# A new whole-kernel order table for sliding-window attention with a convolutional feed-forward: convolution kinds, lead-in and buffers changed with it

## The chip, the cores and the metric

The kernel runs on one core of one Trainium2 chip. The metric is the device time of one execution in microseconds (us), taken on that core. With each execution comes the mean clock that the throttle granted to the matrix engine, as a share of full speed. Engine names follow the profile: PE is TensorE, DVE is VectorE, ACT is ScalarE, POOL is GpSimd, SP is the engine that issues most transfers.

Executions of one kernel differ by up to about 1.4% within a batch here, and the granted clock explains little of it: in the batch of e5 to e8 the unchanged kernel took 227.31 us at a mean clock of 1.000, 227.10 us at 0.992 and 229.90 us at 0.978. Differences under 1% between kernels are therefore not read below. A run more than 1.5% above the fastest of its kernel counts as slow, and is left out of the ratios.

## The reference, cut to what matters

```python
# q, k, v: (8 batches, 8 heads, 576 rows, 64); w_in (512, 1024), conv_w (3, 1024), w_out (1024, 512); float32
def attention(q, k, v):
    scores = q @ k.T / sqrt(64)
    scores = where(abs(i - j) <= 32, scores, -1e9)
    attn = exp(scores - max);  attn /= sum(attn) + 1e-9
    return attn @ v                                  # heads then side by side: x (8, 576, 512)

def ffn(x):
    h = maximum(x @ w_in, 0)
    conv = sum(conv_w[t] * shifted(h, t - 1) for t in range(3))    # along the 576 rows, zeros outside
    return (h / (1 + exp(-conv))) @ w_out            # (8, 576, 512) float32
```

The 8 x 576 rows of the feed-forward are cut into 12 chunks of 384 rows, and its 1024 columns into 8 blocks of 128. A *unit* is one block of one chunk: its matmul, a relu into a buffer `hT`, three *taps* of the convolution, a tanh and a gate. Chunk 1 is done in halves, so there are 104 units.

## The kernel before

The kernel has no scheduler. It describes every operation with what it reads and writes, and a hand-tuned table gives the order, the engine and the buffer of each. Each engine then executes its own instructions in the order of the table, so what stands at the head of a queue holds up all behind it.

```python
BUFS = {'st': 3, 'qkb': 5, 'qkT': 3, 'attn': 2, 'rec': 4, 'xn': 3, 'hT0': 8, 'hT1': 6, 'hT2': 6, 'cp': 2, 'gT': 4, 'y': 7}
CONV = (                     # one letter for each unit, a row for each chunk
    '33333333',
    '33q3323r23223321',
    's222r32q',
    # [...] nine more rows
)
ORDER = """
15D 11D0 12D 1F 17D 2F 13D1 2F 14D 7F 28G 0V 1P0 2F 2V 33V 1F 4G 4F 20G0 21S 2F 16D 5G 1F 22S1 41P120 42P 23S 3G
[...]                        # operation number, engine (D: SP, P, V: DVE, S: ACT, G: GpSimd), buffers; 7F: 7 warming matmuls
"""
TAPS = {                     # kind: taps on (PE, GpSimd, DVE)
    "3": ((0, 1, 2), (), ()), "2": ((0, 2), (), (1,)), "1": ((0,), (), (1, 2)),
    "q": ((), (0, 2), (1,)), "r": ((), (0,), (1, 2)), "s": ((0,), (1, 2), ()),
}
```

The four pieces of code are inside a unit. `hT` and `cp` are in SBUF, `pc` is a bank of PSUM (called `pf` in the profile):

```python
            def emit_times(e_, cp, kk):              # a product on GpSimd: 384 columns, SBUF to SBUF
                gpsimd.tensor_scalar(
                    out=in3(cp.ap), in0=taps(kk), scalar1=w_tap(kk), scalar2=0.0, op0=ALU.mult, op1=ALU.add
                )

            def emit_add(e_, cps=cps):               # kinds q and s: the two products added, on GpSimd
                gpsimd.tensor_tensor(out=in3(cps[0].ap), in0=in3(cps[0].ap), in1=in3(cps[1].ap), op=ALU.add)

            def emit_pc(e_, on_pe=on_pe):            # taps as matmuls with a diagonal, into PSUM
                for kk in on_pe:
                    tensor.matmul(pc.ap[:, 0:nc_], diag_w[:, kk, m, :], taps(kk), ...)

            def emit_tap(e_, kk, from_):             # a tap on DVE; from_ is pc (PSUM) or a product cp (SBUF)
                vector.scalar_tensor_tensor(
                    out=in3(pc.ap), in0=taps(kk), scalar=w_tap(kk), in1=in3(from_.ap), op0=ALU.mult, op1=ALU.add,
                )
```

A unit of kind q costs GpSimd two products and an add, and DVE one tap with two inputs in SBUF (`hT` and `cp`). A unit of kind 2 costs PE two matmuls, and DVE one tap with one input in SBUF (the other is PSUM).

The softmax here doesn't subtract the row's maximum and nothing guards it: scores larger than these inputs give would overflow.

## Time and profile before

| | before |
|---|---|
| time, median of 3 | 227.27 us (227.18 to 227.44) |
| span of the profiled execution | 225.6 us, mean clock 0.991 |
| DVE taps that add a GpSimd product | 35, mean 0.618 us |
| GpSimd products, and adds of two products | 63, mean 0.622 us; 24, mean 1.016 us |
| GpSimd's waits for DVE taps to free a product buffer | 17.0 us |

Columns: line, engine, operation, output<-inputs, shape, count | busy us, mean ns | idle just before, and what ended it.

```profile
L232 POOL TENSOR_SCALAR cp<-hT,conv_w_sb 128x384 f32<-128x384 bf16 (+1 forms) x63 | 38.9, 622 | 46.1 <-ACT hT L232 20.2
...
L232 POOL TENSOR_TENSOR cp<-cp,cp 128x384 f32<-128x384 f32 (+1 forms) x24 | 24.4, 1016 | 1.6
L232 DVE TENSOR_TENSOR attn<-attn,mask 128x1152 bf16<-128x1152 bf16 x26 | 23.0, 886 | 2.4 <-ACT attn L232 2.3
...
L232 DVE SCALAR_TENSOR_TENSOR pf<-hT,conv_w_sb,cp 128x384 f32<-128x384 bf16 (+1 forms) x35 | 21.2, 618 | 0.0
```

The last line is the tap that adds a product: DVE never waits for one (0.0), and the mean of 630 ns for its 33 full-width ones is close to the 613 ns of a full-width tap on PSUM. And from the view of waits of the same kernel (what waited for what: us in total, times, longest):

```profile
POOL cp L232 <- ACT hT L232: 20.2, 10, 4.1
POOL cp L232 <- DVE pf L232: 17.0, 15, 4.2
ACT pf L232 <- DVE pf L232: 11.1, 18, 1.2
```

With only two product buffers, GpSimd stands still 17.0 us until a DVE tap has read a product.

### The profile page before, as it was taken

What the parts mean: (1) busy time and instruction counts of PE and PEld (TensorE: products, weight loads), DVE (VectorE), ACT (ScalarE), POOL (GpSimd) and SP (SyncE); (2) the same over time, 40 slices, a digit from 0 to 9 for tenths busy, and PEclk for the clock granted to TensorE, in tenths of its full rate; (3) what the DMA queues carried; (4) which work ended last, traced back from release to release, by engine and by line L of the source; (5) the groups of instructions that cost most, each with busy time, mean ns of one, the idle gap of its engine ahead of it and who ended that gap; (6) DMA issues with size and microseconds to landing.
All of it is one profiled execution on the core that took longest, in us unless ns stands there. A gap on an engine that the chain in (4) does not pass through costs nothing.

```text
span 225.6 us, 7189 instructions
## 1 busy us (share of the span) xinstructions
PE 211.5 (94%) x2720; PEld 122.9 (54%) x2720; DVE 197.3 (87%) x467; ACT 187.5 (83%) x474; POOL 137.7 (61%) x203
## 2 busy tenths in 40 slices
PE   7698899989989999989999998999999999999993
PEld 5366567658555655545555454545655565455541
DVE  6279869899999979797999788989999999899990
ACT  2689899998989889879889989689989999777642
POOL 5978654654376937695368736756386735566640
PEclk9889999999999999999999999999999999999999
DMA  6999999999989999999997989994535212501224
GB/s 201 331 285 358 355 266 281 321 308 253 290 170 324 317 175 287 236 306 224 288 347 129 202 278 358 182 231 147 144 36 118 99 46 49 175 1 49 93 101 178
DMA packets 66391, 48.16 MB, mean 214 GB/s; under 512 B 50781, under 2 KB 50805, under 8 KB 66357
## 3 DMA queue, kind: packets, MB, share of 16 engines
q1 hardware_dynamic: 64992, 46.32, 78.6%
q10 hardware_dynamic: 1364, 1.39, 2.9%
q8 instruction: 21, 0.34, 0.8%
q14 instruction: 14, 0.11, 0.2%
HBM read 32.52 MB, written 9.44 MB: 186 GB/s over the span
## 4 chain that ended last, share of the span: by engine, by line
PE 41%; DVE 18%; ACT 17%; DMA 13%; issue 5%; SPq 3%; POOL 2%; DVEq 0%; ACTq 0%; POOLq 0%
PE pf L232 41%; DMA st<-in_k_dram 7%; ACT attn L232 6%; DVE pf L232 5%; DVE gT L232 4%; SPq L232 3%; DMA out_dram<-y 3%; ACT xn L232 3%; DVE qkT L232 2%; ACT pf L232 2%; DMA vo<-ve 2%; DVE attn L232 2%; DVE xn L232 2%; ACT qkb L232 2%; ACT y L232 1%
## 5 line engine op out<-in xcount | busy, mean ns | idle before, releaser
L232 PE MATMUL pf<-xT,w_in_sb 128*128 128x385 bf16 (+2 forms) x416 | 73.4, 315 | 3.6 <-ACT hT L232 0.9
L232 PE MATMUL pf<-w_out_sb,gT 128*128 128x512 bf16 x288 | 72.2, 380 | 0.0
L232 POOL TENSOR_SCALAR cp<-hT,conv_w_sb 128x384 f32<-128x384 bf16 (+1 forms) x63 | 38.9, 622 | 46.1 <-ACT hT L232 20.2
L232 ACT ACTIVATE pf<-pf 128x384 f32<-128x384 f32 (+1 forms) x104 | 48.2, 477 | 13.1 <-DVE pf L232 11.1
L232 DVE SCALAR_TENSOR_TENSOR gT<-pf,hT 128x384 bf16<-128x384 f32 (+1 forms) x104 | 52.1, 517 | 5.5 <-ACT pf L232 5.1
L232 PEld LDWEIGHTS <-w_in_sb 128*128 128x128 bf16 x416 | 38.6, 98 | 27.8 <-issue 4.5
L232 ACT ACTIVATE attn<-pf 128x512 bf16<-128x512 f32 (+1 forms) x96 | 41.4, 522 | 1.8 <-PE pf L232 1.8
L232 ACT ACTIVATE hT<-pf 128x385 bf16<-128x385 f32 (+2 forms) x76 | 35.4, 487 | 6.0 <-PE pf L232 5.6
L232 PEld LDWEIGHTS <-gT 128*128 128x128 bf16 x288 | 26.0, 98 | 25.7 <-DVE gT L232 0.5
L232 DVE SCALAR_TENSOR_TENSOR pf<-hT,conv_w_sb,pf 128x384 f32<-128x384 bf16 (+1 forms) x61 | 34.7, 586 | 1.2 <-PE pf L232 1.1
L232 PE MATMUL pf<-hT,diag_w 128*128 128x384 bf16 (+1 forms) x153 | 30.9, 309 | 0.9 <-DVE xn L232 0.6
L232 POOL TENSOR_SCALAR qkb<-st 128x1152 bf16<-128x1152 f32 (+1 forms) x23 | 25.7, 1122 | 7.6 <-DMA st<-in_k_dram 3.2
L232 DVE COPY qkT<-pf 128x576 bf16<-128x576 bf16 x35 | 25.6, 750 | 4.9 <-PE pf L232 4.9
L232 POOL TENSOR_TENSOR cp<-cp,cp 128x384 f32<-128x384 f32 (+1 forms) x24 | 24.4, 1016 | 1.6
L232 DVE TENSOR_TENSOR attn<-attn,mask 128x1152 bf16<-128x1152 bf16 x26 | 23.0, 886 | 2.4 <-ACT attn L232 2.3
L232 ACT ACTIVATE xn<-pf,rec 128x64 bf16<-128x64 f32 x96 | 22.0, 360 | 1.5 <-DVE rec L232 1.5
L232 ACT COPY y<-pf 128x512 f32<-128x512 f32 x30 | 18.1, 605 | 3.9 <-PE pf L232 3.7
L232 DVE SCALAR_TENSOR_TENSOR pf<-hT,conv_w_sb,cp 128x384 f32<-128x384 bf16 (+1 forms) x35 | 21.2, 618 | 0.0
L232 POOL TENSOR_TENSOR attn<-attn,mask 128x1152 bf16<-128x1152 bf16 x6 | 14.2, 2371 | 8.4 <-ACT attn L232 8.4
L232 DVE TENSOR_TENSOR xn<-pf,rec 128x256 bf16<-128x256 f32 x48 | 18.9, 410 | 0.0
L232 ACT COPY qkT<-pf 128x576 bf16<-128x576 bf16 x29 | 18.6, 664 | 0.4 <-PE pf L232 0.2
L232 PEld LDWEIGHTS <-diag_w 128*128 128x128 bf16 x153 | 13.3, 97 | 9.8 <-issue 1.3
(49 smaller groups left out, 235.2 us busy)
## 6 DMA issues: line engine op xcount, KB each, us to landing
st<-in_q_dram SPq DMA_DIRECT2D x16, 576.0 KB, 6.8
out_dram<-y SPq DMA_DIRECT2D x36, 256.0 KB, 3.8
st<-in_k_dram SPq DMA_DIRECT2D x14, 576.0 KB, 8.2
vst<-in_v_dram SPq DMA_DIRECT2D x24, 256.0 KB, 7.0
vst<-in_v_dram SPq DMA_DIRECT2D x15, 192.0 KB, 5.7
vo<-ve SPq DMA_DIRECT2D x11, 260.0 KB, 5.6
st<-in_moe_w_in_dram SPq DMA_DIRECT2D x2, 1024.0 KB, 9.3
st<-in_moe_w_out_dram SPq DMA_DIRECT2D x2, 1024.0 KB, 9.4
```

The lines of the kernel that those rows point to most:

```text
L232: return lambda *args, **kwargs: fixed(do(*args, **kwargs))
```

## The change

The intent is to take work from the three full engines (PE, ACT, DVE) and give it to GpSimd, in a new order with deeper buffers for `hT` and for products. 20 full taps as matmuls and 7 half ones leave PE; units of kind q go from 20 to 36; k casts, v casts and v shifts (copies of a v block from one half of the partitions to the other, `vo` in the profile) go from ACT and DVE to GpSimd; 75 warming matmuls in the lead-in become 4. The numbers of nearly all operations change too, because the table is renewed from its first line to its last.

```diff
-BUFS = {'st': 3, 'qkb': 5, 'qkT': 3, 'attn': 2, 'rec': 4, 'xn': 3, 'hT0': 8, 'hT1': 6, 'hT2': 6, 'cp': 2, 'gT': 4, 'y': 7}
-TURNS = ('eeeee', 'eeede', 'eeeed', 'dedde', 'ddddd', 'ddddd', 'ddddd', 'edddd')
+SPLIT = (1,)
+BUFS = {'st': 3, 'qkb': 5, 'qkT': 3, 'attn': 2, 'rec': 6, 'xn': 2, 'hT0': 9, 'hT1': 9, 'hT2': 9, 'cp': 8, 'gT': 3, 'y': 4}
+TURNS = ('eeeee', 'eedde', 'eeeed', 'deddd', 'ddddd', 'ddddd', 'ddddd', 'ddddd')
+MASKS = ('mm', 'mm', 'mm', 'mm', 'mm', 'mm', 'mm', 'mm')
 CONV = (
-    '33333333',
-    '33q3323r23223321',
-    's222r32q',
-    [... nine more rows]
+    '13qr1312',
+    '13qq223r2332232r',
+    'q222332q',
+    [... nine more rows]
 )
 ORDER = """
-15D 11D0 12D 1F 17D 2F 13D1 2F 14D 7F 28G 0V 1P0 2F 2V 33V 1F 4G 4F 20G0 21S 2F 16D 5G 1F 22S1 41P120 42P 23S 3G
-[... 86 more lines]
+11D0 12D 15D 17D 13D1 0V 14D 1P0 2V 7V 18D 20V0 22V1 23V 21G 28G 4G 41P120 42P 6V 45P34 46P 16D 19D 48S 47V 30G 44V
+[... 86 more lines]
 """
+    outside = sb.tile([128, 128], BF16, name="outside")
+    gpsimd.memset(outside, 0.0)
+    [... four affine_select: a constant for masks added by matmul; MASKS takes that route for no unit]
@@ a unit's product buffers
-                op(f"cp {at} {kk} {kind_}", [...], acquire=[cp], use=[hT], **of)
+                o = op(f"cp {at} {kk} {kind_}", [...], acquire=[] if begun else cps, use=[hT] + cps, behind=begun, **of)
```

The rest of the diff generalizes the cutting of chunks without changing what is computed.

## The prediction

> **What bounds the kernel now.** I read the busy shares, then three stretches, then the chain of waits, then the groups.
>
> The busy shares and the head of the chain:
>
> ```profile
> PE 211.5 (94%) x2720; PEld 122.9 (54%) x2720; DVE 197.3 (87%) x467; ACT 187.5 (83%) x474; POOL 137.7 (61%) x203
> ...
> PE 41%; DVE 18%; ACT 17%; DMA 13%; issue 5%; SPq 3%; POOL 2%; DVEq 0%; ACTq 0%; POOLq 0%
> ```
>
> Three engines are nearly full and GpSimd is the one with room. PE's 94% overstates it, because each matmul is shown with its pipeline's tail. The starts of back-to-back matmuls in the trace lie 0.216 us apart for 512 columns, 0.164 for 384 to 386, 0.083 for 192, and about 0.016 for the paired 64-column ones. Summed this way PE has 179.7 us of useful work, 80% of the span. DVE, ACT and GpSimd instructions overlap their neighbours a little too; counted start to start I get DVE 184.5, ACT 176.2, GpSimd 126.8 us. These "spacings" are used below.
>
> I mark stages by the last output matmul of sequence chunks 0, 5 and 11 (52.1, 148.8, 221.7 us; found by counting w_out matmuls):
>
> ```profile
> 8.40:52.10 43.70, 40.86 (x649) 27.15 (x651) 35.64 (x88) 41.17 (x110) 28.66 (x47) 0.96 1.12 312
> 52.10:148.80 96.70, 92.43 (x1325) 53.18 (x1325) 88.62 (x209) 84.88 (x213) 62.94 (x68) 1.00 1.07 255
> 148.80:221.70 72.90, 72.40 (x718) 38.77 (x715) 68.66 (x149) 58.73 (x149) 40.47 (x52) 1.00 0.35 99
> ```
>
> Columns: stretch and length, then busy us of PE, weight load, DVE, ACT, POOL, then clock, DMA share, GB/s. The first stage is ACT's, the middle is shared by DVE, PE and ACT, the last is PE's (69.2 us of useful matmul time by spacing in 72.9, 95%), with DVE behind it. Until 148.8 us the DMA share is above 1.
>
> The chain shows the same change of hands. Columns: start, length, what:
>
> ```profile
> 1.83 6.50 DMA st<-in_k_dram
> 8.36 0.63 ACT qkb L232
> ...
> 83.06 4.46 DMA vo<-ve
> ...
> 109.73 8.84 DMA st<-in_k_dram
> ...
> 136.25 48.21 PE pf L232 x603
> ...
> 194.01 27.28 PE pf L232 x142
> ```
>
> The reader should see that the start waits on the first k load, that a few transfers come into the chain in the middle, and that from 136 us on it is PE nearly alone.
>
> **What the Trainium skill says.** "Perfetto Trace Analysis", section "Identifying the Most-Contended Engine", warns that matmul busy time is not a measure of nearness to the limit; the 211.5 shown against 179.7 by spacing agrees.
>
> "TensorE: Matmul & The Clock Gate", part 1 on the HAM clock gate: the array idles at half clock and is released by about 3.4 us of activity. The trace agrees: the warming matmuls (256 columns on a tile of zeros) start 0.213 us apart until 6.2 us and again from 10.0 to 13.1 us, and 0.109 apart after.
>
> "SBUF — State Buffer", section "Who interferes with whom": a DVE instruction with two SBUF inputs and a GpSimd instruction that reads SBUF exclude each other, and the later one waits. The trace agrees (start, length):
>
> ```profile
> 63.68 1.14 POOL L232 TENSOR_SCALAR qkb<-st 128x1152 bf16<-128x1152 f32 x1
> 63.70 1.73 DVE L232 TENSOR_TENSOR attn<-attn,mask 128x1152 bf16<-128x1152 bf16 x1
> 64.79 1.11 POOL L232 TENSOR_SCALAR ve<-vst 128x512 bf16<-128x512 f32 x1
> ```
>
> The mask multiply takes 0.75 us undisturbed; here it takes 1.73, behind the cast.
>
> "GPSIMD Engine Reference", section 3.1: two-input elementwise work runs at its read port's rate, much slower than one-input. Here the add of two 384-column products takes 1.0 us undisturbed, one product 0.58.
>
> **The change, part by part.** I matched every operation of the two order tables by kind and engine.
>
> PE loses work. The convolution kinds move from "taps as diagonal matmuls" to "taps on GpSimd": full-width tap matmuls 118 to 98, half-width 35 to 28: 20 x 0.163 + 7 x 0.083 = 3.9 us. Three of the turns of x (10 matmuls of 0.057) go to DMA transposes: 0.6 us. PE: 179.7 - 4.4 = 175.1 with rounding. The 75 warming matmuls become 4; they are extra.
>
> DVE loses 15 copies of the turned q and k out of PSUM: 15 x 0.665 = 10.0 us; three sums (1.4) and two relus (0.9). It gains casts and diagonals (3.2 + 1.2), four normalizing multiplies (1.3), two output copies (1.2), one turn copy (0.6) and 0.3 of taps. One fewer v cast saves 0.3. DVE: 184.5 to about 179.6.
>
> ACT takes those 15 copies (15 x 0.53 = 8.0) and two relus (0.8), and gives up casts (5.9 of k, 1.1 of q, 2.0 of v, 1.5 of w_out), four turn copies (1.7), four normalizing groups (3.2) and two output copies (1.0): 176.2 to 168.5.
>
> GpSimd gets 25 more products (13.6), 13 more adds (12.4), 7 more v shifts, three of them whole blocks at 1.9 (8.3), k, v and w_out casts (9.1), less q and w_in casts (2.2) and half its diagonals (4.2): 126.8 to 163.8. A new constant that no operation uses (no unit takes the added-mask route) costs one memset and four selects, near 1 us by the 0.24 us of a select, before its first cast.
>
> DMA: 11 to 7 copies of v blocks and 29 to 33 transposes. By packet times over 16 engines a copy is 13.4/11 = 1.2 us and a transpose 15.8/29 = 0.55, so 4.9 - 2.2 = 2.7 us less of some 186.
>
> By stage, largest sums by spacing: the first had ACT 39.6 in 43.7 us; it will have DVE 35.5 and ACT 35.5 with GpSimd 33.1. The middle had DVE 84.3 in 96.7; it will have PE 82.1, DVE 81.6. The last had PE 69.2 in 72.9; it will have PE 68.2, DVE 62.5, GpSimd 56.8.
>
> On the path: the first q and k are now issued ahead of v; that v block is about 0.25 MB at the 232 GB/s of the first 8.4 us, so 1.0 us earlier. First stage: 4.1 less of its largest sum, but three engines now stand within 2.4 us of each other so I keep only half, and charge 1 us for a cold PE (9 us of PE work fall before 30 us, mostly beside other work): -1.1. Middle: 96.7 x 82.1/84.3 = 94.2, -2.5. Last: 72.9 x 68.2/69.2, -1.1. The ending gets 0.3 longer: nine output matmuls after the last gate become seven (-0.4), but with 4 output buffers in place of 7 the last copies wait for stores of chunk 10 to land (3.8 us from issue), which I put at +0.7. Added exclusion between DVE and GpSimd: 15 more products-plus-tap instructions with two SBUF inputs, at a busier GpSimd; the 26 masks of before average 0.886 us against 0.75 undisturbed, 3.5 us in all, and a third more gives about +1, of which half counts: +0.5. Sum: -1.0 - 1.1 - 2.5 - 1.1 + 0.3 + 0.5 = -4.9. So 227.3 - 4.9 = 222.4 us, 2.1% less.
>
> **The rivals.** (1) GpSimd becomes the bound. It is at 164 us by spacing, some 77% of the working time, and what waits for it (two products, an add, then the tap) is a serial 2.1 us per unit. For: q units go from 20 to 36. Against: hT rises from 20 buffers to 27 and the product buffers from 2 to 8, which lets it run well ahead, and no stage has it as the largest sum. It would eat the gain: 225 to 229. (2) Transfers are the bound until 148 us. For: a DMA share of 1.07 to 1.12 and, after the first load, 19 us of transfers on the chain (the two above and a store of 6.0). Against: the engines' waits on loads come to some 22 us, spread over three engines with short ones, and SP's own waits are for compute. Then only 2.7 us of DMA time come off, and the result is 224 to 225. (3) The reordering closes holes that sums cannot see: before, the middle stage had 12 us in which its busiest engine idled. The deeper hT and product buffers speak for it. A third of those holes is another 4 us: 218. (4) The cold clock reaches into the first FFN chunk; each 3.4 us of half clock there costs up to 1.7 us: 224 to 226.
>
> **Range and chances.** Sums put the centre just over the 2% line (222.7). Rival 3 pulls down, 1, 2 and 4 up; the main engines all have less to do, so a loss would need GpSimd to turn out the bound. 217.5 to 226.5. Faster by over 2%: 0.53; within 2%: 0.44; slower: 0.03.
>
> **What would show it.** Right: PE matmuls fall to about 2612 (108 fewer: 71 warming, 37 others), DVE busy down by 5, ACT by 8, GpSimd up to about 175 us busy; the gain shared over all stages with the middle largest; chain after 136 us still PE. First ACT or DVE cast near 7.4 us. Clock below full in more of the first 25 us. Wrong: waits of DVE taps for cp running to more than 5 us in all would mean rival 1; loads at the head of the waits, rival 2; a middle stage under 91 us, rival 3; half clock past 30 us, rival 4.

## The result, and the profile after

The changed kernel is correct and slower: 237.67 us median of 4 runs (237.21 to 239.71), against 227.36 us for the kernel before on the same chip (227.18 to 230.82; the last is a slow run). The ratio is 1.0473 with a 95% interval of 1.0397 to 1.055. Ratios here and below are the mean time of one kernel's fast runs over that of the other's of the same rounds, so they are not quite the ratio of the medians.

The page of the changed kernel: busy shares, then the head of the chain that ended last.

```profile
PE 202.2 (86%) x2585; PEld 116.8 (50%) x2612; DVE 211.4 (90%) x471; ACT 179.7 (76%) x454; POOL 191.4 (81%) x257
...
DVE 30%; POOL 28%; PE 22%; issue 8%; ACT 6%; DMA 4%; POOLq 1%; SPq 0%; DVEq 0%; ACTq 0%
```

PE has 2612 weight loads, 108 fewer, exactly as counted (27 of its matmul records are missing). ACT fell by 7.8 us as expected. But DVE, which should have lost 5 us, has 14.1 us *more*, and PE has gone from 41% of the chain to 22%, with DVE and GpSimd in its place. The groups that answer to those shown of before:

```profile
L234 POOL TENSOR_SCALAR cp<-hT,conv_w_sb 128x384 f32<-128x384 bf16 (+1 forms) x88 | 61.4, 706 | 13.8 <-ACT hT L234 7.1
...
L234 DVE SCALAR_TENSOR_TENSOR pf<-hT,conv_w_sb,cp 128x384 f32<-128x384 bf16 (+1 forms) x50 | 39.6, 796 | 5.9 <-POOL cp L234 3.7
...
L234 POOL TENSOR_TENSOR cp<-cp,cp 128x384 f32<-128x384 f32 (+1 forms) x37 | 39.7, 1075 | 1.4
...
L234 DVE TENSOR_TENSOR attn<-attn,mask 128x1152 bf16<-128x1152 bf16 x26 | 24.3, 941 | 1.4 <-ACT attn L234 1.3
```

The same tap now takes 796 ns instead of 618, and the same product 706 instead of 622. Their shapes have not changed. The waits:

```profile
ACT pf L234 <- DVE pf L234: 19.4, 24, 2.5
POOL cp L234 <- ACT hT L234: 7.1, 7, 2.0
...
DVE pf L234 <- POOL cp L234: 3.7, 5, 1.1
```

GpSimd's 17.0 us of waiting for DVE are gone (there are 8 product buffers), and DVE waits only 3.7 us for products. What grew is ACT's wait for DVE taps, 11.1 to 19.4 us. So the view of waits does not show the cause: an instruction that is held up by another engine *after* it has started is booked as busy.

The last stage in the chain of the changed kernel (start, length, what):

```profile
192.34 6.10 POOL cp L234 x8
...
198.61 1.90 POOL cp L234 x2
...
205.06 6.32 POOL cp L234 x9
...
212.26 10.53 POOL cp L234 x14
...
229.09 1.90 PE pf L234 x8
```

Before, this was PE alone (the 27.28 us piece in the prediction). Now GpSimd's products and adds stand one behind another until the last matmuls.

To see where the time went I took the moment at which each chunk's last output weight load ends (the gaps between these ends are lengths of stages; they end within 0.6 us of the stages that the prediction marks):

| stage, us | before | changed | predicted change |
|---|---|---|---|
| start to chunk 0 | 51.6 | 57.1 | -2.1 (lead-in and first) |
| chunk 0 to chunk 5 | 96.7 | 95.9 | -2.5 |
| chunk 5 to chunk 11 | 73.0 | 78.2 | -1.1 |
| to the end of the span | 4.4 | 4.6 | +0.3 |

In the profiled execution of the changed kernel the granted clock was 0.57 from 51.5 to 55.5 us, which may take up some of the first line's loss; this comes back below. The first matmul of the feed-forward comes at 26.0 us (25.8 before), so the lead-in (all that comes before it) neither won nor lost.

### The profile page after: what moved, and what is told of

The parts are those of the page before. It is cut to its first block, busy times and chain, and to the rows that moved or that the text cites. A ratio compares the mean times of both kernels' runs of the same rounds, so it can differ in the third digit from the quotient of the medians.

```text
span 235.7 us, 6946 instructions
## 1 busy us (share of the span) xinstructions
PE 202.2 (86%) x2585; PEld 116.8 (50%) x2612; DVE 211.4 (90%) x471; ACT 179.7 (76%) x454; POOL 191.4 (81%) x257
## 4 chain that ended last, share of the span: by engine, by line
DVE 30%; POOL 28%; PE 22%; issue 8%; ACT 6%; DMA 4%; POOLq 1%; SPq 0%; DVEq 0%; ACTq 0%
PE pf L234 22%; POOL cp L234 19%; DVE pf L234 9%; DVE gT L234 5%; DVE attn L234 4%; POOL vo L234 3%; DMA st<-in_q_dram 2%; POOL qkb L234 2%; DVE hT L234 2%; DVE ve L234 2%; POOL ve L234 2%; DVE xn L234 2%; DMA vst<-in_v_dram 2%; DVE qkT L234 2%; ACT hT L234 1%
## 5 line engine op out<-in xcount | busy, mean ns | idle before, releaser
L234 POOL TENSOR_SCALAR cp<-hT,conv_w_sb 128x384 f32<-128x384 bf16 (+1 forms) x88 | 61.4, 706 | 13.8 <-ACT hT L234 7.1
L234 ACT ACTIVATE pf<-pf 128x384 f32<-128x384 f32 (+1 forms) x104 | 46.4, 468 | 21.9 <-DVE pf L234 19.4
L234 DVE SCALAR_TENSOR_TENSOR pf<-hT,conv_w_sb,cp 128x384 f32<-128x384 bf16 (+1 forms) x50 | 39.6, 796 | 5.9 <-POOL cp L234 3.7
L234 POOL TENSOR_TENSOR cp<-cp,cp 128x384 f32<-128x384 f32 (+1 forms) x37 | 39.7, 1075 | 1.4
L234 ACT COPY qkT<-pf 128x576 bf16<-128x576 bf16 x44 | 27.2, 656 | 8.4 <-PE pf L234 6.5
L234 DVE SCALAR_TENSOR_TENSOR pf<-hT,conv_w_sb,pf 128x384 f32<-128x384 bf16 (+1 forms) x48 | 26.8, 570 | 1.0 <-PE pf L234 0.7
L234 PE MATMUL pf<-hT,diag_w 128*128 128x384 bf16 (+1 forms) x126 | 25.9, 311 | 1.7 <-DVE gT L234 0.6
L234 POOL TENSOR_SCALAR ve<-vst 128x512 bf16<-128x512 f32 x25 | 18.6, 751 | 5.3 <-DMA vst<-in_v_dram 5.2
L234 PE MATMUL pf<-ve,attn 128*64 128x65 bf16 x320 | 17.4, 203 | 4.2 <-DVE gT L234 1.7
L234 PEld LDWEIGHTS <-attn 128*64 128x64 bf16 x576 | 13.7, 116 | 13.8 <-issue 9.1
L234 PE MATMUL pf<-qkT 64*128 64x64 bf16 x576 | 15.5, 196 | 5.4 <-ACT qkT L234 3.5
```

Source lines behind the costliest of these rows:

```text
L234: return lambda *args, **kwargs: fixed(do(*args, **kwargs))
```

## The experiments

The theories that I set against each other: the loss comes from GpSimd's added load, either because DVE taps and GpSimd instructions exclude each other (X) or simply because GpSimd's in-order queue is too long and delivers late (O); or it comes from something else in the new order, such as the cold lead-in. Where an edit cuts the columns of a product the result is wrong; the tolerance of the comparison is wide enough that some of these still count as correct.

### First group: undoing parts in place

Three runs put back the convolution kinds of before (their PE, GpSimd and DVE operations replaced at the same places of the order), for chunks 0 and 1, for chunks 8 to 11, and for all:

```diff
 CONV = (
-    '13qr1312',
-    '13qq223r2332232r',
+    '33333333',
+    '33q3323r23223321',
     [... e1; e2 does the same with the last four rows, e3 with all twelve]
```

> The changed kernel with the conv kinds of chunks 0 and 1 as they were before (12 units; their GpSimd products and adds go, diagonal matmuls come back at the same places of the order), all else as changed. Theory G (GpSimd is the engine that binds wherever it carries products, casts and shifts together): the last output matmul of chunk 0, 57.1 us in the changed kernel against 51.6 before, comes back to 53 to 54, and the time falls from 237.7 to about 234. Theory H (the new order and the smaller buffers are at fault, not the kinds): chunk 0 still ends at 56 to 57 us and the time stays within 1.5 us of 237.7.

> The changed kernel with the conv kinds of chunks 8 to 11 as before (21 units), all else as changed. Theory G: the stretch from the end of chunk 5 to the end of chunk 11, 78.2 us in the changed kernel against 73.0 before, falls to 73 to 75, the time to about 233 to 234. Theory H: the stretch stays at 77 to 79 us and the time within 1.5 us of 237.7.

> The changed kernel with every conv kind as before (55 units), the new order otherwise, casts and shifts still moved to GpSimd. Theory G: most of the loss goes, 228 to 231, DVE busy falls from 211 to below 200 and GpSimd from 191 to about 160. Theory H: 235 or more.

Measured: e1 237.12 us (ratio to before 1.0373, 1.0309 to 1.0438), e2 246.0 us (1.0771), e3 261.38 us (1.1458). GpSimd's busy time fell as it should, to 185.1, 171.3 and 154.4 us, yet e2 and e3 are far slower, and e1 stays within the 1.5 us that theory H gave it. Two of the waits of e2 have grown, from 19.4 and 7.1 us in the changed kernel:

```profile
ACT pf L232 <- DVE pf L232: 30.7, 27, 3.8
POOL cp L232 <- ACT hT L232: 30.0, 16, 6.4
```

My reading, which no run shows by itself, is that a matmul put at the place where a product had stood holds up PE's queue until its relu is done, and that the wait goes round through ACT to GpSimd: an order is fitted to its assignment of engines, and undoing a part in place disturbs the rest. So I take these runs to decide nothing about the cause, and the next ones leave every operation on its engine and change only what it costs.

### Second group: what GpSimd's products cost

In e4 a product or add reads 8 columns of each half and fills the rest by memset, which keeps GpSimd occupied but takes its reads away. In e5 the memset goes too, after one filling of each buffer. e6 is the cut of e5 in the kernel before.

```diff
 # e4
-    out=in3(cp.ap), in0=taps(kk), scalar1=w_tap(kk), scalar2=0.0, op0=ALU.mult, op1=ALU.add
+    out=in3(cp.ap)[:, :, 0:8], in0=taps(kk)[:, :, 0:8], scalar1=w_tap(kk), scalar2=0.0,
+    op0=ALU.mult, op1=ALU.add,
 )
+gpsimd.memset(in3(cp.ap)[:, :, 8:], 0.01)
 # e5, e6: as e4 without the last line, and the add cut likewise
```

> Wrong result on purpose. The changed kernel with each GpSimd product and add replaced by a read of 8 columns and a memset over the rest, so that GpSimd is occupied for nearly as long but hardly reads SBUF while it works. Theory X (inside G: the loss is the exclusion between GpSimd's reads and DVE instructions with two SBUF inputs): the tap that adds a product falls from a mean of 0.80 us to 0.62 to 0.65, the product and add of GpSimd to their undisturbed length, and the time falls by 5 us or more. Theory O (inside G: GpSimd's queue is simply too long): the taps get shorter but the time falls by less than 2.5 us as long as GpSimd's products and adds last about as long as undisturbed ones (0.58 and 1.0 us).

> Wrong result on purpose. The changed kernel, same order, same instructions and waits, but every GpSimd product and add of the convolution works on 8 columns of each half only, so GpSimd's share for them falls from about 100 us to about 35 and the exclusion with it. Theory G (GpSimd's load, queue and exclusion together, is the whole loss): the time falls to 227 or less, and both the end of chunk 0 (57.1 us) and the last stretch (78.2 us) shrink by 3 us or more. Theory H (the new order, cold lead-in and buffers): the time stays at 233 or more.

> Control, wrong result on purpose. The kernel before with the same cut of its GpSimd products and adds. If GpSimd does not bind there, as its trace says (two thirds busy, no chain through it), the time falls by at most 2 us from 227.4. If it falls by 5 us or more, then freeing GpSimd speeds any of these orders and the run before does not tell the two kernels apart.

Measured: e4 234.39 us (1.0269, 1.0202 to 1.0335), e5 228.72 us (0.9999, 0.9925 to 1.0073), e6 227.37 us (0.9945, 0.9869 to 1.0021). The same cut brings back the whole loss in the new order and nothing in the old. So the loss is in GpSimd's load. The groups of e4, then the busy shares and groups of e5:

```profile
L234 POOL MEMSET cp<- 128x368 f32 (+2 forms) x162 | 62.6, 401 | 2.2
...
L234 POOL TENSOR_SCALAR cp<-hT,conv_w_sb 128x16 f32<-128x16 bf16 (+1 forms) x88 | 31.8, 361 | 17.0 <-ACT hT L234 8.8
...
L234 DVE SCALAR_TENSOR_TENSOR pf<-hT,conv_w_sb,cp 128x384 f32<-128x384 bf16 (+1 forms) x50 | 36.5, 733 | 7.3 <-POOL cp L234 4.1
```

```profile
PE 202.0 (89%) x2612; PEld 116.6 (51%) x2612; DVE 202.6 (89%) x471; ACT 179.4 (79%) x454; POOL 130.4 (57%) x265
...
L234 POOL TENSOR_SCALAR cp<-hT,conv_w_sb 128x16 f32<-128x16 bf16 (+1 forms) x88 | 29.5, 343 | 54.6 <-ACT hT L234 43.9
...
L234 DVE SCALAR_TENSOR_TENSOR pf<-hT,conv_w_sb,cp 128x384 f32<-128x384 bf16 (+1 forms) x50 | 35.0, 705 | 3.5 <-POOL cp L234 0.7
```

The memsets of e4 leave the tap nearly as it is without them (733 against 705 ns), although they hold GpSimd for 62.6 us: writing alone hardly holds up a tap. But e4 is 5.7 us slower than e5, so an occupied queue costs time as well. This pair does not separate X from O, and e4 has its own flaw: with its memsets GpSimd works for longer on products than in the changed kernel.

### Third group: the lead-in

e7 puts back the 75 warming matmuls; e8 leaves out the constant that nothing uses.

```diff
 # e7
-11D0 12D 15D 17D 13D1 0V 14D 1P0 2V 7V 18D [...]
+12F 11D0 12D 15D 17D 13D1 0V 14D 1P0 10F 2V 7V 18D [...]
 # e8
-    gpsimd.memset(outside, 0.0)
-    [... and the four affine_select]
```

> The changed kernel with the 75 warming matmuls of before put behind the same PE operations of the lead-in (in place of its 4). If the cold clock costs time (half clock until 24.5 us in the changed kernel), the first FFN matmul comes before 25 us and the time falls by 1 us or more. If the lead-in is bound by DVE, ACT and GpSimd, as the first FFN matmul at 26.0 us against 25.8 before suggests, the time stays within 0.7 us.

> The changed kernel without building the constant that no operation uses (one memset and four selects on GpSimd, which stood against the DVE's mask copies: the identity copy ends at 4.7 us against 3.8 before). If the lead-in's start counts, the time falls by 0.5 to 1 us; if the first loads or the later GpSimd queue hide it, it stays the same within 0.4 us.

Measured: e7 238.22 us (1.0417), e8 237.86 us (1.038): neither moves the time. Chunk 0 ended 1.7 and 1.3 us earlier in their profiles, which I first read as a gain in the lead-in that was lost later. That reading was wrong: neither of these two executions has the stretch at half clock that the changed kernel's has between 51.5 and 55.5 us. At a mean clock of 0.57 those 4 us lose 0.43 x 4 = 1.7 us of PE's time, which would account for it. Why their last stages are longer than the changed kernel's (79.5 and 79.6 us against 78.2) stays open.

### Fourth group: moves to other engines, and the order of before

e9 gives one product of each of the 36 q units to ACT; e10 gives ten casts of the first chunks to ACT and ten v shifts to DVE; e11 gives chunks 8 to 11 of the kernel before the kinds of the changed one (with 4 product and 5 output buffers), and e12 is its control, with these buffers alone.

```diff
 # e9: the engine of 36 entries of the order, as
-301G01
+301S01
 # with, in emit_times:
+    if e_ == "S":
+        scalar.activation(in3(cp.ap), taps(kk), AF.Copy, bias=0.0, scale=w_tap(kk))
+        return
 # e10: 20 entries, as
-28G [...] 154G
+28S [...] 154V
 # e11 and e12, in the kernel before
-[...] 'cp': 2, 'gT': 4, 'y': 7}
+[...] 'cp': 4, 'gT': 4, 'y': 5}
```

> The changed kernel with one of the two GpSimd products of each of its 36 q units computed on ACT at the same place of the order (correct result). GpSimd loses about 20 us of work, ACT gains about 17 to 18 and comes back to what it had before. Theory G: the time falls by 3 to 6 us from 237.7, and the mean of the taps that add a product falls below 0.75 us. If instead GpSimd's queue is not what binds, ACT's longer queue makes it slower or leaves it the same within 1 us.

> The changed kernel with GpSimd's side work of the lead-in moved off it at the same places of the order: 4 w_out casts, 4 v casts and 2 k casts to ACT, 10 small v shifts to DVE. Theory G says the early part is bound by GpSimd's casts, shifts and products together, so the end of chunk 0 (57.1 us) falls to 54 or less and the time by 2 to 3 us. If the products alone are at fault, or DVE and ACT are as full there, chunk 0 still ends after 56 us.

> The other way round: the kernel before with the changed kernel's conv kinds in chunks 8 to 11 (21 units changed; more q), 4 product buffers and 5 output buffers so that it fits. Theory G: the last stretch, 73.0 us, grows by 3 us or more and the time to 231 or more. Theory H: it stays within 1.5 us of its control e12.

> Control for e11: the kernel before with 4 product buffers and 5 output buffers in place of 2 and 7, kinds and order untouched. Expected within 0.7 us of the kernel before (227.4); a loss of more than 1.5 us would say that output buffers matter.

Measured: e9 242.4 us (1.0698), e10 245.75 us (1.0859), both slower than the changed kernel (for e9 the second of the two cases foreseen, for e10 a miss); e11 241.86 us (1.0648; its profiled run was slow), e12 227.71 us (1.0096). e11 is slower than 231 us, as theory G had it, but like e2 it changes units in place, so I don't count it. The table of e12 still gives the products only two of the four buffers (GpSimd waits 17.5 us for taps, as before), so e12 tests fewer output buffers and not deeper product buffers. In e9 GpSimd's adds now wait 26.4 us for ACT's half of the sum. In e10 a cast comes to stand before a load that has not landed, and a shift behind it:

```profile
POOL vo L232 <- ACT ve L232: 8.3, 1, 8.3
ACT L232 <- DMA vst<-in_v_dram: 7.7, 1, 7.7
```

That is the queue effect of the first group again. e11 says that 21 more GpSimd-heavy units cost the old order 14 us, which fits the load theory, but it carries the same stalls.

### Fifth group: exclusion by itself

The prediction was wrong by far and X against O was still open. In e13 (wrong) only the DVE tap changes: its second tensor is the PSUM bank instead of the product, and the product enters as one number per partition. So the tap still waits for the product and takes as long, but has one tensor input in SBUF. Every queue, wait and GpSimd instruction stays. e18 is the control, the same edit in the kernel before.

```diff
-    out=in3(pc.ap), in0=taps(kk), scalar=w_tap(kk), in1=in3(from_.ap), op0=ALU.mult, op1=ALU.add,
+    out=in3(pc.ap), in0=taps(kk), scalar=w_tap(kk) if inside else from_.ap[:, 0:1], in1=in3(pc.ap),
+    op0=ALU.mult, op1=ALU.add,          # inside: from_ is pc
```

> The changed kernel, wrong on purpose: where a VectorE tap adds a GpSimd product, it now takes the accumulator bank in PSUM as its second tensor and the product only as one number per partition. So the 50 taps have one SBUF tensor instead of two, while GpSimd's products, adds and casts, every wait and every queue stay as they are. Theory X (the mutual exclusion of two-input DVE work and GpSimd is the loss): the mean of a tap falls from 0.80 to about 0.62 us, GpSimd's products come down from 0.71 towards 0.62, and the time falls by 5 us or more, to 233 or less. Theory O (GpSimd's queue is simply too long, its products come too late whoever excludes whom): taps may shorten, but the time falls by 3 us at most, to 235 to 238.

> Control of e13: the kernel before with the same edit of its 35 taps that add a product (wrong on purpose). Their mean is 0.62 us already and the exclusion that its trace shows for them is 0.7 us in all, with 2.5 us for the products. So it should stay within 1.5 us of before, 226 to 228; if it falls by 4 us or more, the edit itself saves time and e13 says less about exclusion.

Measured: e13 228.71 us (1.0081, 0.9975 to 1.0186) and e18 229.17 us (1.0048, 0.9982 to 1.0114; relative errors 0.12 and 0.11, as meant). The edit takes 9.0 us off the changed kernel's 237.67 and nothing off the kernel before. Busy shares of e13, the head of its chain and its groups, and then the tap in e18:

```profile
PE 198.5 (88%) x2585; PEld 115.6 (51%) x2612; DVE 202.5 (90%) x471; ACT 178.9 (79%) x454; POOL 178.1 (79%) x257
...
PE 59%; DVE 18%; POOL 9%; issue 5%; DMA 4%; ACT 3%; POOLq 0%; DVEq 0%
...
L234 POOL TENSOR_SCALAR cp<-hT,conv_w_sb 128x384 f32<-128x384 bf16 (+1 forms) x88 | 52.9, 611 | 16.7 <-ACT hT L234 10.6
...
L234 POOL TENSOR_TENSOR cp<-cp,cp 128x384 f32<-128x384 f32 (+1 forms) x37 | 37.1, 1004 | 1.4
L234 DVE SCALAR_TENSOR_TENSOR pf<-hT,cp,pf 128x384 f32<-128x384 bf16 (+1 forms) x50 | 29.8, 601 | 4.2 <-POOL cp L234 2.3
```

```profile
L232 DVE SCALAR_TENSOR_TENSOR pf<-hT,cp,pf 128x384 f32<-128x384 bf16 (+1 forms) x35 | 20.6, 601 | 0.0
```

The tap is back at 601 ns, and GpSimd's products, whose instructions were not touched, are back from 706 to 611 ns. PE leads the chain again. Directly, the taps lose 39.6 - 29.8 = 9.8 us on DVE, and products and adds (61.4 + 39.7) - (52.9 + 37.1) = 11.1 us on GpSimd. One clash, as the timeline of the changed kernel shows it on DVE and on GpSimd (start, length):

```profile
205.04 1.44 DVE L234 SCALAR_TENSOR_TENSOR pf<-hT,conv_w_sb,cp 128x384 f32<-128x384 bf16 x1
...
205.06 0.99 POOL L234 TENSOR_TENSOR cp<-cp,cp 128x384 f32<-128x384 f32 x1
```

and the same tap of e13, beside three products:

```profile
198.31 0.61 DVE L234 SCALAR_TENSOR_TENSOR pf<-hT,cp,pf 128x384 f32<-128x384 bf16 x1
...
198.35 1.71 POOL L234 TENSOR_SCALAR cp<-hT,conv_w_sb 128x384 f32<-128x384 bf16 x3
```

In the first, both start within 0.02 us of each other and the tap, though its record starts first, ends 0.43 us after the add. In the second they run side by side at their own speed.

The end of e13's chain is PE again, where the changed kernel had products one behind another:

```profile
191.25 10.20 PE pf L234 x56
201.50 9.49 PE pf L234 x49
211.04 10.33 PE pf L234 x49
```

So X holds. O is not a rival of X so much as its second half: exclusion makes GpSimd's instructions longer, and the lengthened queue is what stands in the chain. A comparison of e13 with e5 bears this out: both end at 228.7 us with DVE busy for 202.5 and 202.6 us, although GpSimd is busy for 178.1 us in the one and 130.4 in the other. So it is not GpSimd's own occupation that sets the time here.

e15 asks whether load alone hurts the order of before: each of its 63 products is issued twice, with the same result.

```diff
                 gpsimd.tensor_scalar(out=in3(cp.ap), in0=taps(kk), [...])
+                gpsimd.tensor_scalar(out=in3(cp.ap), in0=taps(kk), [...])
```

> The kernel before with every one of GpSimd's 63 products issued twice (same values, same result): GpSimd's work by spacing goes from 127 to about 162 us, where the changed kernel has 164; all else is the same. If GpSimd's load alone (queue and exclusion) explains the loss, this is slower than before by several us, 231 to 238, with masks and taps of DVE longer. If an order fitted to its GpSimd load is needed to lose, it stays within 1.5 us of before.

Measured: 253.32 us (1.115, 1.1048 to 1.1253), far beyond the 231 to 238 that the load theory gave. Its waits:

```profile
ACT pf L232 <- DVE pf L232: 36.4, 33, 5.5
DVE pf L232 <- POOL cp L232: 21.7, 23, 2.2
```

With two product buffers the doubled product stands directly ahead of the tap, and DVE now does wait for GpSimd, 21.7 us. The taps themselves grew to 826 ns as well. At a GpSimd busy time of 182.3 us, under the changed kernel's 191.4, this is much slower. That suggests that the changed kernel's order and deep buffers do absorb a late product and not exclusion; e15 alone does not show it.

### Sixth group: where the loss sits

e14 is e5 without its extra memsets in the lead-in (the first use of each buffer is done in full instead); e16 cuts the products in chunks 6 to 11 alone; e17 is e13 with the lead-in edits of e7 and e8 together.

```diff
 # e14; e16 has SHORT = (6, 7, 8, 9, 10, 11)
+    wiped, SHORT = set(), (0, 1, 2, 3, 4, 5, 6, 7, 8, 9, 10, 11)
[...]
+                full = c not in SHORT or cp.index not in wiped
+                a_ = lambda ap: ap if full else ap[:, :, 0:8]
```

> The changed kernel, wrong on purpose: GpSimd's products and adds work on 8 columns only, as in e5, but the first use of each product buffer is done full, so that no extra memsets are needed in the lead-in (they took 3.4 us there in e5). If e5's memsets hid part of the gain, this run ends about 3 us before e5, at 225 to 226, and chunk 0 ends near 53; if the lead-in gains are lost again later as in e7 and e8, it ends within 1.5 us of e5, at 227.5 to 230.

> As e14, but only the units of chunks 6 to 11 have the short products and adds. It splits e5's gain of 9 us: if the late stage holds the loss of its own, this run gets about 5 us (232 to 233); if the late loss is only the early one carried on, 1 us at most (236 to 237); if nearly all of the gain is late, 229 to 230.

> Wrong on purpose, as e13 (each tap takes PSUM in place of the product), and with the two lead-in parts of e7 and e8 undone as well: 75 warming matmuls as before, and the unused constant not built. e7 brought the end of chunk 0 forward by 1.7 us and e8 by 1.3 us, and both lost it again in the rest. If the rest lost it because of exclusion, chunk 0 now ends near 52.5 and the whole at 225 to 226, 2 to 3 us under e13. If the lead-in is worth nothing for another reason, it ends at 227.5 to 229 as e13.

Measured: e14 229.72 us (1.0113, 1.0000 to 1.0226), as e5; e16 232.83 us (1.0227, 1.0126 to 1.0327), so of e14's 8 us some 5 come from chunks 6 to 11 and 3 from the earlier ones, each uncertain by about 2 us; e17 230.81 us (1.0155, 1.0091 to 1.0219), a miss: no gain over e13, and rather 2 us more. e17's executions had mean clocks of 0.983 to 0.992, e13's 0.997 to 1.000. The means differ by 0.011, which could be worth 2.5 us at most, and the profiled execution of e17 has the half-clock stretch again (0.61 from 51.5 to 55.5 us) and ends chunk 0 only at 57.6 us. So I read e17 as "the lead-in edits are worth nothing". The intervals of e14, e16 and e17 all include 2%, so the record classes the three as unclear against the kernel before.

The stages again, from the profiled executions (us):

| stage | before | changed | e13 | e14 |
|---|---|---|---|---|
| start to chunk 0 | 51.6 | 57.1 | 54.9 | 55.9 |
| chunk 0 to 5 | 96.7 | 95.9 | 92.7 | 93.6 |
| chunk 5 to 11 | 73.0 | 78.2 | 73.9 | 74.3 |
| to the end | 4.4 | 4.6 | 4.6 | 4.6 |

Without exclusion at the taps the middle does become shorter, by 4.0 us, and the last stage falls to within 0.9 us of before. The first stage stays 3.3 us longer, and e14, with hardly any product work, does not mend it either; nor does e1, which takes the moved products out of chunks 0 and 1 and ends chunk 0 at 54.9 us as e13 does. The chain of e13 from 28 to 49 us is mostly GpSimd's queue, with casts of q, k and v (`qkb`, `ve`) and shifts of v (`vo`) among products. It begins:

```profile
28.01 1.15 POOL qkb L234
29.16 1.14 POOL cp L234 x2
...
30.37 0.99 POOL cp L234
...
31.46 0.67 POOL vo L234
...
32.23 0.58 POOL cp L234
32.81 1.13 POOL qkb L234
```

That points at the casts and shifts that the new order gives to GpSimd there. It is argued from the chain, not shown: the run that tried to move them (e10) stalled on loads, and the cause of these 3.3 us stays open.

No version beat the kernel before. e13 and e5, which compute something wrong, are the best of the new order, and they only equal it.

## Why the prediction was wrong

By its own steps:

**The work that was removed: right.** 108 fewer PE instructions, ACT down by 7.8 us (8 predicted), and the middle stage's gain of work is real: with the tap exclusion gone (e13) it is 4.0 us shorter, where 2.5 were predicted.

**"Added exclusion between DVE and GpSimd ... +0.5": the step that failed.** The clash between taps and GpSimd alone measured 9.0 us (changed kernel to e13), or by stages of the profiled executions 2.2, 3.2 and 4.3 us; most of the first may be the half-clock stretch that e13's execution lacks, since e7 and e8, which lack it too, end chunk 0 only 0.5 and 0.8 us after e13. The term was sized from the 26 masks and raised by a third. What it left out are the taps and, above all, the other side: the product that comes second waits as well. Counting for each operation, operands and shape what its instructions take beyond the length that a tenth of them stay under (summed from the traces), DVE's excess went from 9.8 to 25.0 us and GpSimd's from 7.6 to 24.4; full-width taps with a product hold 9.3 of the first (0.7 before), full-width products 12.1 of the second (2.4 before). In e13 these sums are 16.0 and 11.0.

**The rival that came true in part, and why it was dismissed.** "GpSimd becomes the bound", given 225 to 229 us, was set aside because `hT` and product buffers let "it run well ahead". GpSimd did come to stand in the chain, but by exclusion and not by its own work, and the size was missed too (237.67). My reading is that running ahead made it worse. Before, with two product buffers, GpSimd stood still while DVE read its product: the 17.0 us of waits shown above; 28 of the 35 taps began with GpSimd idle. With eight buffers GpSimd is often at its next product when the tap begins: only 9 of the 50 taps begin with GpSimd idle, and 24 start while a product runs (6 of 35 before). That the shallow buffers protected the taps is how I read the two traces; no run changed the buffers of the new order alone. What is shown is that the clash between taps and products is worth 9 us in the one order and nothing in the other (e13, e18).

**"DVE: 184.5 to about 179.6", "busy down by 5".** It rose by 14.1 us. e13 takes 8.9 of that away. A part of the rest is the masks (0.94 us on average against 0.89) and the v casts on DVE (0.77 against 0.45), which the prediction left at their lengths of before. Three of the seven v casts meet a GpSimd instruction, take 1.06 to 1.37 us and end 0.28 to 0.29 us after it; the other four take 0.42. A v cast has one SBUF input, so clashes are not confined to two-input instructions. No run takes these away, and what they cost the kernel is not shown.

**"GpSimd up to about 175 us busy".** It was 191.4; in e13, 178.1. The estimate was nearly right for a GpSimd that the taps do not hold up.

**The last stage, "-1.1".** +5.2 us. "No stage has it as the largest sum" was true of GpSimd's undisturbed work (56.8 us) and false of what it took: it was busy for 68.57 of the 81.20 us of that stage, DVE for 75.20:

```profile
148.80:230.00 81.20, 74.52 (x725) 39.31 (x735) 75.20 (x147) 61.56 (x153) 68.57 (x79) 1.00 0.35 98
```

**The first stage, "-1.1" and the lead-in's "-1.0".** The loads of q and k do come earlier: the casts of the first k block end at 7.8 us, against 9.6 before. But the first feed-forward matmul did not, and the stage lost 3.3 us even in e13. Neither fewer warming matmuls nor the unused constant is the cause (e7, e8, e17); GpSimd's queue is the likely one, and it stays open.

**The ending, "+0.3".** 4.6 against 4.4 us: right.

**The sign that was to show rival 1 did not.** I had named "waits of DVE taps for cp running to more than 5 us". They came to 3.7 us. Exclusion does not appear as a wait; it appears as a longer mean of the same shape. The sign should have been a tap's mean over, say, 0.7 us. Half clock past 30 us, the sign of rival 4, was there (51.5 to 55.5 us), but e7 and e8 are as slow as the changed kernel and their profiled executions lack it.

What the Trainium skill said was enough to see it: "SBUF — State Buffer", section "Who interferes with whom", has the exclusion, with the loser fully blocked and either side able to lose, and the runs agree, with e13 (one SBUF input: 601 ns) and e4 (a GpSimd that mostly writes: 733 ns against 705) on its finer points. "Perfetto Trace Analysis", section "Optimizing Scalar/DVE Operations", warns that GpSimd and DVE share a read port, "so offloading operations between those two might not help"; the 9 us are its size here. I used the rule for the masks, where the trace of before showed it, and not for the instructions that the change multiplied.

## What to carry to other kernels

Before giving work to GpSimd, count the DVE instructions with two SBUF inputs that will run beside it, look at its one-input casts as well, and charge both engines for the clashes; the tap with its second input from PSUM was free of it here (601 ns). Look for exclusion in the mean length of one shape, not in the waits. Undoing one part of a tuned in-order table in place made it slower still here (e2 and e3): change what an operation costs instead, and leave it where it is.

## What the Trainium skill lacked or had wrong

- "SBUF — State Buffer", section "Who interferes with whom": it gives the rule and says that issue order decides who is blocked, but not how that looks in a profile. Here the blocked instruction counts as busy: the tap's mean rose from 618 to 796 ns, while DVE's waits for products showed only 3.7 us.
- The same section gives no sizes for a mix of real instructions. At a GpSimd that is 81% busy, 50 two-input taps cost 9.0 us of 237.67, by e13.
- "GPSIMD Engine Reference", section 4.1 "Engine selection": its row on elementwise work compares the two engines alone. It lacks that the result, read by DVE beside another SBUF tensor, then makes a two-input instruction: product and tap were 706 and 796 ns together, 611 and 601 ns when the tap's second tensor was in PSUM.
- "TensorE: Matmul & The Clock Gate", part 1: it ties half clock after the warm-up to idle gaps of PE and puts the ramp at under 1% of a typical span. The size agrees (71 fewer warming matmuls moved the first feed-forward matmul from 25.8 to only 26.0 us). What it lacks is that the later stretches come and go between executions. The changed kernel's had the clock at 0.57 from 51.5 to 55.5 us although PE was idle for at most 1.3 us at a time between 40 and 58 us; e7's, with an idle stretch of the same 1.3 us, had full clock there. The kernel before had mean clocks of 0.978 to 1.000 in one batch. So a single profile that holds such a stretch can mislead by up to 1.7 us in a stage, as it did me in e7 and e8.
